# Spectral input of a two-layer GFNet kernel: five transposes of 128 columns, a plain copy of z, statistics one tile ahead

## The chip, the cores and the metric

The kernel runs on one core of a Trainium2 chip. Its time is the device time of one execution in microseconds (us), and lower is better. Three runs of the kernel before took 770.5, 771.51 and 773.9 us; the median is 771.51. The engines are called PE (TensorE; its weight loads, PEld, run beside its matmuls), DVE (VectorE), ACT (ScalarE), POOL (GpSimd) and SP (SyncE, which here only issues DMAs). Each engine works through its own queue of instructions in order.

## The reference

The input x has 2048 rows of 576 columns in bf16. Two layers are computed one after the other, each with its own residual additions:

```python
x = x + A(layernorm(x))          # spectral mixer
x = x + B(layernorm(x))          # MLP, which normalises its input once more

def A(x):   # X: 2048 x 289 complex
    X = rfft2(x) ; X = X * (w_r + 1j * w_i)
    return irfft2(X, s=(2048, 576))

def B(x):
    y = layernorm(x)
    return gelu(y @ w1 + b1) @ w2 + b2      # 576 -> 4608 -> 576
```

Both layers use the same weights. The transforms are done as matrix products with constant cosine and sine matrices.

## The kernel before

All of x stays in SBUF as 16 tiles; tile t holds the rows 16p + t on its 128 partitions p. The two-dimensional transform is done in factors. The real transform along the 576 columns comes first, tile by tile. The transform along the 2048 rows is split into 16 x 128 (in the code 8 and 16 inside a tile, then an exchange between partitions, then the rest). All instructions keep the order in which the program writes them down on each engine: a manual schedule is set for PE, ACT, DVE and POOL.

The class `SpectralIn` (from line 298) is the part that is changed. For each tile it does this:

- `fold` (lines 304 to 308): DVE adds and subtracts the two halves of the 576 columns, 288 each, into a buffer xf of two rows of 320. The sum serves the even frequencies, the difference the odd ones.
- Statistics: `ln_bn_one` (line 265) takes two batch statistics of 288 columns and one aggregation on DVE. `ln_scale` (line 271) makes 1/sqrt(variance + eps) from them. In the first stage ACT takes the square root (line 277) for two tiles at a time and DVE the reciprocal (line 280). In the MLP it is a chain of small DVE operations for one tile. The mean needs no subtraction at this place.
- `turn` (line 314): six PE transposes of 96 columns each (line 319), and one ACT copy of the 96 x 768 result out of PSUM (line 321) into xT.
- `dft_d` (line 324): six matmuls with 290 moving columns (line 329), three for the even and three for the odd frequencies, against the constant c_fd. ACT copies the result z (line 334), multiplies it by the row's 1/sqrt, and at the same time interleaves even and odd frequencies, writing every second element.
- `dft_v` (line 341): four matmuls (lines 344 to 347) with the constant c_k1 as weights and z as the moving operand, into two PSUM rows, real and imaginary. ACT (line 350) or DVE (line 352), in turn, copies the result to y1, which has 5 buffers.
- `exchange` (line 380): SP issues one DMA that spreads y1 over 8 partitions of the array vx. A buffer of y1 is free again when its DMA has read it.

The method `run_all` (line 356) is the first stage of layer 0. In iteration i it does `turn` of tile i-1, `dft_v` of tile i-4, `dft_d` of tile i-2, `fold` of tile i, then the statistics of tile i, and with every second tile the square root and the reciprocal of that pair. Constants and weights for the following stage are loaded by POOL (line 211) in the same iterations; each load waits for the `turn` copy of a given tile.

After this stage come `middle` (line 389: the second row factor, the multiplication by w, and the first factor of the way back), `SpectralOut` (line 450: the rest of the way back and the residual addition) and `mlp` (line 672). `middle` begins with a matmul that reads vx, so it needs all exchanges.

Layer 1's spectral input isn't a stage of its own. In the MLP of layer 0, `mlp_down` (line 652) finishes the rows of one tile after another, and calls hooks after every sixth of its matmuls' groups; `fold`, `turn`, `dft_d` and `dft_v` of the tile before are put into these hooks. So 15 tiles are worked on between MLP matmuls. The sixteenth follows after the last MLP matmul, with filler matmuls (`keep_busy`, line 202) between its steps.

Of the kernel before, what the change touches and what calls it, by code (L numbers as in the profile page):

```python
# [10 lines left out]
ACT = mybir.ActivationFunctionType  # L11
ALU = mybir.AluOpType
BF16 = mybir.dt.bfloat16
F32 = mybir.dt.float32
# [7 lines left out]
S, D = 2048, 576  # L22
P = 128
NT = 16
DH = D // 2
KH = 145
KP = 2 * KH
# [10 lines left out]
ENGINES = [getattr(mybir.EngineType, n) for n in ("PE", "Activation", "DVE", "Pool")]  # L38


def _fd():
    d = np.arange(DH)[:, None].astype(np.float64)
    j = np.arange(KH)[None, :].astype(np.float64)
    halves = []
    for odd in range(2):
        ang = 2 * np.pi * d * (2 * j + odd) / D
        re, im = np.cos(ang), -np.sin(ang)
        dead = KH - 1 if odd else 0
        re[:, dead] = 0
        im[:, dead] = 0  # L50
        halves.append(np.concatenate([re, im], axis=1).reshape(3, 96, KP))
    return np.concatenate(halves, axis=0).transpose(1, 0, 2)


def _k1():
# [61 lines left out]
def kernel(  # L117
# [12 lines left out]
    nc = tc.nc  # L130
# [5 lines left out]
    persist = ctx.enter_context(tc.tile_pool(name="persist", bufs=1))  # L136
    arena = ctx.enter_context(tc.tile_pool(name="arena", bufs=1))
    shared = ctx.enter_context(tc.tile_pool(name="shared", bufs=1))
    work = ctx.enter_context(tc.tile_pool(name="work", bufs=2))
# [5 lines left out]
    def uid():  # L145
        _n[0] += 1
        return _n[0]

    def big_ps(shape, dtype=F32):
        return ps_big.tile(shape, dtype, tag="big", name=f"psb{uid()}")  # L150

    def sm_ps(shape, dtype=BF16):
        return ps_sm.tile(shape, dtype, tag="sm", name=f"pss{uid()}")
# [13 lines left out]

    x_sb = persist.tile([P, NT, D], BF16, name="x_sb")
    ident = persist.tile([P, P], BF16, name="ident")
    c_fd = persist.tile([96, 6, KP], BF16, name="c_fd")  # L170
    c_k1 = persist.tile([P, 3, P], BF16, name="c_k1")
    c_f2 = persist.tile([P, 16, 3, P], BF16, name="c_f2")
    c_r1 = persist.tile([P, 2, 256], BF16, name="c_r1")
# [14 lines left out]
    order = [t for q in QUADS for t in q]  # L188
# [11 lines left out]
    marks = {}  # L200
# [64 lines left out]
    def ln_bn_one(mv, t):  # L265
        stats = work.tile([P, 2, nc.vector.BN_STATS_DIM], F32, tag="ln_stats")
        for h in range(2):
            nc.vector.bn_stats(out=stats[:, h, :], in_=x_sb[:, t, h * DH : (h + 1) * DH])  # L268
        nc.vector.bn_aggr(out=mv, in_=stats[:])  # L269

    def ln_scale(mv, mlp, sqrt):

        n = mv.shape[1]
        rs = work.tile([P, n], F32, tag="ln_rs", bufs=4)
        if sqrt:
            sq = work.tile([P, n], F32, tag="ln_v")
            nc.scalar.activation(
                out=sq[:], in_=mv[:, :, 1], func=ACT.Sqrt, bias=c_eps[:, 1:2] if mlp else c_eps[:, 0:1], scale=(1.0 + EPS) if mlp else 1.0
            )
            nc.vector.reciprocal(out=rs[:], in_=sq[:])  # L280
            return [(mv[:, i, 0:1], rs[:, i : i + 1]) for i in range(n)]

        vv = work.tile([P, n], F32, tag="ln_v")
        hv = work.tile([P, n], F32, tag="ln_hv")
        tt = work.tile([P, n], F32, tag="ln_t")
        sc, add = (1.0 + EPS, EPS * EPS) if mlp else (1.0, EPS)
        nc.vector.tensor_scalar(out=vv[:], in0=mv[:, :, 1], scalar1=sc, scalar2=add, op0=ALU.mult, op1=ALU.add)
        nc.vector.tensor_scalar(out=hv[:], in0=vv[:], scalar1=-0.5, scalar2=None, op0=ALU.mult)
        nc.vector.tensor_scalar(
            out=rs[:].bitcast(I32), in0=vv[:].bitcast(I32), scalar1=-0.5, scalar2=1597463007.0, op0=ALU.mult, op1=ALU.add  # L290
        )
        for _ in range(3):
            nc.vector.tensor_mul(out=tt[:], in0=rs[:], in1=rs[:])
            nc.vector.tensor_mul(out=tt[:], in0=tt[:], in1=hv[:])
            nc.vector.scalar_tensor_tensor(out=rs[:], in0=tt[:], scalar=1.5, in1=rs[:], op0=ALU.add, op1=ALU.mult)
        return [(mv[:, i, 0:1], rs[:, i : i + 1]) for i in range(n)]

    class SpectralIn:
# [3 lines left out]
            self.vx, self.st, self.sqrt = vx, {}, sqrt  # L302

        def fold(self, t, odd_engine):
            xf = work.tile([P, 2, 320], BF16, tag="xn", bufs=3)
            nc.vector.tensor_tensor(out=xf[:, 0, 0:DH], in0=x_sb[:, t, 0:DH], in1=x_sb[:, t, DH:D], op=ALU.add)  # L306
            odd_engine.tensor_tensor(out=xf[:, 1, 0:DH], in0=x_sb[:, t, 0:DH], in1=x_sb[:, t, DH:D], op=ALU.subtract)
            self.st["xf", t] = xf

        def stats(self, tiles):  # L310
# [2 lines left out]

        def turn(self, t):
            xf = self.st.pop(("xf", t))
            pt = sm_ps([P, 6, P])
            for o in range(2):
                for ci in range(3):
                    nc.tensor.transpose(pt[0:96, 3 * o + ci, :], xf[:, o, 96 * ci : 96 * ci + 96], ident[:])  # L319
            xT = work.tile([96, 6, P], BF16, tag="turn")  # L320
            marks["turn", t] = nc.scalar.copy(out=xT[:], in_=pt[0:96]).ins  # L321
            self.st["xT", t] = xT

        def dft_d(self, t):
            xT = self.st.pop(("xT", t))
            pz = big_ps([P, 2, 512])
            for o in range(2):
                for ci in range(3):
                    nc.tensor.matmul(  # L329
                        pz[:, o, 0:KP], lhsT=xT[:, 3 * o + ci, :], rhs=c_fd[:, 3 * o + ci, :],  # L330
                        start=(ci == 0), stop=(ci == 2),
                    )
            z = work.tile([P, 2, KP], BF16, tag="z", bufs=3)
            nc.scalar.activation(
                out=z[:].rearrange("p r (j o) -> p r o j", o=2),
                in_=pz[:, :, 0:KP].rearrange("p o (r j) -> p r o j", r=2),
                func=ACT.Copy, scale=self.st.pop(("rs", t)),
            )
            self.st["z", t] = z

        def dft_v(self, t, on_act):
            z = self.st.pop(("z", t))
            py = big_ps([P, 2, 512])
            nc.tensor.matmul(py[:, 0, 0:KP], lhsT=c_k1[:, 0, :], rhs=z[:, 0, :], start=True, stop=False)
            nc.tensor.matmul(py[:, 0, 0:KP], lhsT=c_k1[:, 2, :], rhs=z[:, 1, :], start=False, stop=True)
            nc.tensor.matmul(py[:, 1, 0:KP], lhsT=c_k1[:, 0, :], rhs=z[:, 1, :], start=True, stop=False)
            nc.tensor.matmul(py[:, 1, 0:KP], lhsT=c_k1[:, 1, :], rhs=z[:, 0, :], start=False, stop=True)
            y1 = work.tile([P, 2, KP], BF16, tag="y1", bufs=5)
            if on_act:
                ins = nc.scalar.copy(out=y1[:], in_=py[:, :, 0:KP]).ins  # L350
            else:
                ins = nc.vector.tensor_copy(out=y1[:], in_=py[:, :, 0:KP]).ins
            marks["y1", t] = ins
            exchange(self.vx, t, y1[:])

        def run_all(self, loads):
            for i in range(NT + 4):
                if 0 <= i - 1 < NT:
                    self.turn(order[i - 1])
                if 0 <= i - 4 < NT:  # L360
                    self.dft_v(order[i - 4], on_act=(i % 2 == 0))
                if 0 <= i - 2 < NT:
                    self.dft_d(order[i - 2])
                if i < 4:
                    keep_busy((5, 1, 1, 1)[i])
                if i < NT:
                    t = order[i]
                    self.fold(t, nc.vector)
                    if i % 2 == 0:
                        mv = work.tile([P, 2, nc.vector.BN_AGGR_DIM], F32, tag="ln_mv", bufs=4)  # L370
                    ln_bn_one(mv[:, i % 2, :], t)
                    if i % 2 == 1:
                        for tt, (_, rs) in zip(order[i - 1 : i + 1], ln_scale(mv, False, self.sqrt)):
                            self.st["rs", tt] = rs
                for call in loads.get(i, ()):
                    call()

# [160 lines left out]
    class Prep:  # L538
# [14 lines left out]
        def moments(self):  # L553
            mean = work.tile([P, 4], F32, tag="ln_hv")
            var = work.tile([P, 4], F32, tag="ln_v")
            sq = work.tile([P, 4], F32, tag="ln_t")
            nc.vector.tensor_scalar(out=mean[:], in0=self.s12[:, 0], scalar1=1.0 / D, scalar2=None, op0=ALU.mult)
            nc.vector.tensor_mul(out=sq[:], in0=mean[:], in1=mean[:])
            nc.vector.scalar_tensor_tensor(out=var[:], in0=self.s12[:, 1], scalar=1.0 / D, in1=sq[:], op0=ALU.mult, op1=ALU.subtract)
            self.mean, self.var = mean, var  # L560
# [157 lines left out]
    for n, (kind, j) in enumerate(first[:-3]):  # L718
        i = 1 + max(n - 1, 0)
# [72 lines left out]
```

## Time and profile before

| what | us |
|---|---|
| median of three runs (lowest, highest) | 771.51 (770.5, 773.9) |
| the profiled execution's own time | 772.16 |
| its span, first to last instruction | 770.4 |
| PE busy | 743.6 |
| ACT busy | 341.8 |
| DVE busy | 256.9 |
| first spectral stage, to the first matmul of `middle` | 0 to 46.5 |
| stretch with layer 1's spectral tiles inside the MLP | from about 150 to 412.9 |
| last tile of layer 1's spectral input, to the first matmul of `middle` | 414.8 to 423.2 |

Busy time is the sum over an engine's instructions, counted once where they overlap. The granted TensorE clock was full during the whole span. A row of the order of work shows the start, the duration, the engine, the line of the code, the operation, what it writes and reads, and in square brackets the idle time of the engine before it with what ended that idle time. A duration counts from start to end of one instruction; instructions of one engine overlap somewhat, so the distance between starts is what a queue of them costs.

### The profile page before, as it was taken

How to read it: one execution, taken by the hardware profiler on the slowest of the kernel's cores; microseconds unless marked ns; L12 is line 12 of the kernel's file. 1: busy time of each engine (PE TensorE's matmuls, PEld its weight loads, DVE VectorE, ACT ScalarE, POOL GpSimd, SP SyncE). 2: the span in 40 equal slices, each digit the busy share in tenths (PEclk: the TensorE clock that was granted, in tenths of full speed). 3: DMA queues.
4: the chain of work that ended last, by engine and by line, in shares of the span. 5: the costliest groups of instructions: out<-in, count | busy, mean ns of one | idle time of the engine just before them, and what ended most of it. 6: DMA issues, size and time to landing. Idle time of an engine off the chain costs nothing. (4 is left out here: it accounts for less than half of the span.)

```text
span 770.4 us, 12539 instructions
## 1 busy us (share of the span) xinstructions
PE 743.6 (97%) x5207; PEld 464.6 (60%) x5207; DVE 256.9 (33%) x843; ACT 341.8 (44%) x561; POOL 39.8 (5%) x75
## 2 busy tenths in 40 slices
PE   8879999999999999999999898999999999999997
PEld 5645744785478547854686565458646854784476
DVE  5855960245024602330133959201400140010011
ACT  6956855324542464236422866641154035204600
POOL 3320011000000000000004000100000000000000
PEclk9999999999999999999999999999999999999999
DMA  7844935000000000000004510620000000000000
GB/s 225 223 129 163 260 97 181 2 16 9 1 9 17 9 1 9 17 9 1 9 11 143 162 48 1 199 77 17 16 0 8 17 9 0 9 16 9 0 17 16
DMA packets 22377, 41.61 MB, mean 54 GB/s; under 512 B 4292, under 2 KB 15376, under 8 KB 22320
## 3 DMA queue, kind: packets, MB, share of 16 engines
q0 software_dynamic: 5696, 22.57, 9.7%
q1 hardware_dynamic: 16224, 17.76, 7.7%
q8 instruction: 41, 0.67, 0.4%
q10 hardware_dynamic: 400, 0.47, 0.2%
q14 instruction: 16, 0.13, 0.1%
HBM read 28.93 MB, written 2.36 MB: 41 GB/s over the span
## 5 line engine op out<-in xcount | busy, mean ns | idle before, releaser
L660 PEld LDWEIGHTS <-h_sb 128*128 128x128 bf16 x2304 | 223.8, 98 | 56.7
L618 PEld LDWEIGHTS <-w_sb 128*128 128x128 bf16 x1152 | 108.7, 98 | 145.8 <-issue 22.6
L590 DVE TENSOR_SCALAR xn<-x_sb,mv,rs 128x576 bf16<-128x576 bf16 x24 | 9.4, 427 | 198.1 <-PE pss_6918 L600 33.8
L268 DVE BATCH_NORM_STATS2 stats<-x_sb 128x6 f32<-128x288 bf16 x112 | 44.7, 440 | 0.0
L626 PEld LDWEIGHTS <-w1r_sb 64*128 64x128 bf16 x288 | 10.2, 94 | 26.0 <-issue 20.3
L656 DVE TENSOR_TENSOR xb<-x_sb,b_bc 128x576 f32<-128x576 bf16 x32 | 24.0, 749 | 0.0
L329 PEld LDWEIGHTS <-xT 96*128 96x128 bf16 x192 | 19.3, 101 | 7.0 <-ACT xT L321 0.7
L593 POOL COPY xn<-xn 128x64 bf16<-128x64 bf16 x24 | 5.8, 253 | 335.7 <-DVE xn L590 335.5
L319 PEld LDWEIGHTS <-xf 128*96 128x96 bf16 x192 | 15.4, 131 | 11.2 <-DVE xf L306 10.6
L428 PEld LDWEIGHTS <-h_sb 128*128 128x128 bf16 x128 | 12.0, 96 | 14.3 <-issue 9.5
L398 PEld LDWEIGHTS <-c_f_80 128*128 128x128 bf16 x128 | 12.3, 97 | 9.4 <-issue 5.1
L668 DVE TENSOR_TENSOR x_sb<-psb_7445,xb 128x576 bf16<-128x576 f32 x1 | 0.8, 758 | 43.6 <-PE psb_7445 L660 43.6
L668 DVE TENSOR_TENSOR x_sb<-psb_4074,xb 128x576 bf16<-128x576 f32 x1 | 0.8, 758 | 41.6 <-PE psb_4074 L660 41.6
L206 PEld LDWEIGHTS <-zeros 128*128 128x128 bf16 x86 | 8.5, 102 | 10.0 <-DVE h_sb L224 1.0
L211 POOL DMA_DIRECT2D h_sb<-in_A_w_r_dram x8 | 6.0, 750 | 133.3 <-issue 103.6
L269 DVE BATCH_NORM_AGGREGATE mv<-stats 128x2 f32<-128x12 f32 x56 | 11.7, 209 | 1.9
L600 PEld LDWEIGHTS <-xn 128*128 128x128 bf16 x160 | 11.5, 98 | 1.4
L632 ACT ACTIVATE h_sb<-psb_5977,b_sb 128x512 bf16<-128x512 f32 x2 | 1.3, 684 | 23.7 <-PE psb_5977 L626 23.7
L632 ACT ACTIVATE h_sb<-psb_7209,b_sb 128x512 bf16<-128x512 f32 x2 | 1.3, 684 | 23.7 <-PE psb_7209 L626 23.7
L632 ACT ACTIVATE h_sb<-psb_6593,b_sb 128x512 bf16<-128x512 f32 x2 | 1.3, 684 | 23.7 <-PE psb_6593 L626 23.7
L548 ACT ACTIVATE h_sb<-x_sb 128x576 bf16<-128x576 bf16 x16 | 11.0, 686 | 0.1
L306 DVE TENSOR_TENSOR xf<-x_sb 128x288 bf16<-128x288 bf16 x32 | 9.6, 299 | 4.1 <-DMA x_sb<-in_A_x_dram 4.1
(1353 smaller groups left out, 1478.4 us busy)
## 6 DMA issues: line engine op xcount, KB each, us to landing
w_sb<-in_B_w_dram SPq DMA_DIRECT2D x16, 288.0 KB
v_sb<-in_B_w_dram POOLq DMA_DIRECT2D x4, 1152.0 KB, 6.6
h_sb<-const_i POOLq DMA_DIRECT2D x8, 384.0 KB, 5.9
shared_1445<-in_B_w_dram POOLq DMA_DIRECT2D x2, 1440.0 KB, 7.3
shared_5356<-in_B_w_dram POOLq DMA_DIRECT2D x2, 1440.0 KB, 7.8
b_sb<-shared_704 SPq DMA_DIRECT2D x16, 145.0 KB
v_sb<-shared_4643 SPq DMA_DIRECT2D x16, 145.0 KB
h_sb<-in_A_w_r_dram POOLq DMA_DIRECT2D x8, 289.0 KB, 4.4
```

The costliest lines, as they stand in the source:

```text
L268: nc.vector.bn_stats(out=stats[:, h, :], in_=x_sb[:, t, h * DH : (h + 1) * DH])
L269: nc.vector.bn_aggr(out=mv, in_=stats[:])
L319: nc.tensor.transpose(pt[0:96, 3 * o + ci, :], xf[:, o, 96 * ci : 96 * ci + 96], ident[:])
L329: nc.tensor.matmul(pz[:, o, 0:KP], lhsT=xT[:, 3 * o + ci, :], rhs=c_fd[:, 3 * o + ci, :], start=(ci == 0), stop=(ci == 2),)
L398: nc.tensor.matmul(px[:, o, 0:KP], lhsT=c_f2[:, e, pl, :], rhs=vx[:, e, ri, :], start=(q == 0), stop=(q == 1))
L428: nc.tensor.matmul(ph[:, o, 0:KP], lhsT=i1[:, n % 4, pl, :], rhs=xp[:, ri, :], start=(q == 0), stop=(q == 1))
L548: nc.scalar.activation(out=at(h_sb, [P, D], 512 * 34), in_=x_sb[:, self.quad[i], :], func=(ACT.Copy, ACT.Square)[k], accum_out=self.s12[:, ...
L600: nc.tensor.transpose(pt[:, ci, :], xn[:, ci * 128 : (ci + 1) * 128], ident[:])
L618: nc.tensor.matmul(ph[:, q, :], lhsT=w1_sb[:, ci, fc * 128 : (fc + 1) * 128], rhs=yT[:, ci, :], start=(first and ci == 0), stop=(not first ...
L626: nc.tensor.matmul(acc[p][:, q, :], lhsT=w1r_sb[rows, p, :], rhs=yT[rows, 4, :], start=first, stop=not first)
L656: nc.vector.tensor_tensor(out=xb[:], in0=xr, in1=b2_bc[:].rearrange("p (h n) -> p h n", h=2), op=ALU.add)
L660: nc.tensor.matmul(po[:, h, 0:DH], lhsT=hts[fc][:, i * 128 : (i + 1) * 128], rhs=w2_chunk(fc)[:, h * DH : (h + 1) * DH], start=(fc == 0), ...
```

## The change

`fold` now writes xf as one run of 576 columns, sums then differences. `turn` transposes it in five pieces of 128 columns, at 0, 128, 256, 384 and 448; the last two overlap by 64 columns. The third piece holds both even and odd columns, so both groups of three matmuls in `dft_d` read it. The constant c_fd grows from 96 to 128 partitions and has zeros where a piece holds columns of the other half, or columns already counted.

The copy of z in `dft_d` keeps the order of PSUM: even frequencies, then odd ones, each with real and imaginary part. The moving operand of `dft_v` now reads z with an inner step of 290 elements (even, odd) and an outer step of 1. The output is the same interleaved order as before.

In `run_all` the fold of tile i comes directly after the transposes of tile i-1; after it, with every second tile, come the square root and the reciprocal; then `dft_v` and `dft_d`; and at the end of the iteration the statistics of tile i+1.

```diff
+CHUNKS = ((0, 0), (128, 0), (256, 0), (384, 0), (448, 64))
+HALF_CHUNKS = ((0, 1, 2), (2, 3, 4))
...
-    c_fd = persist.tile([96, 6, KP], BF16, name="c_fd")
+    c_fd = persist.tile([P, 6, KP], BF16, name="c_fd")
...
-            xf = work.tile([P, 2, 320], BF16, tag="xn", bufs=3)
-            nc.vector.tensor_tensor(out=xf[:, 0, 0:DH], in0=x_sb[:, t, 0:DH], in1=x_sb[:, t, DH:D], op=ALU.add)
-            odd_engine.tensor_tensor(out=xf[:, 1, 0:DH], in0=x_sb[:, t, 0:DH], in1=x_sb[:, t, DH:D], op=ALU.subtract)
+            xf = work.tile([P, 640], BF16, tag="xn", bufs=3)
+            nc.vector.tensor_tensor(out=xf[:, 0:DH], in0=x_sb[:, t, 0:DH], in1=x_sb[:, t, DH:D], op=ALU.add)
+            odd_engine.tensor_tensor(out=xf[:, DH:D], in0=x_sb[:, t, 0:DH], in1=x_sb[:, t, DH:D], op=ALU.subtract)
...
-            pt = sm_ps([P, 6, P])
-            for o in range(2):
-                for ci in range(3):
-                    nc.tensor.transpose(pt[0:96, 3 * o + ci, :], xf[:, o, 96 * ci : 96 * ci + 96], ident[:])
-            xT = work.tile([96, 6, P], BF16, tag="turn")
-            marks["turn", t] = nc.scalar.copy(out=xT[:], in_=pt[0:96]).ins
+            pt = sm_ps([P, 5, P])
+            for ci, (start, _) in enumerate(CHUNKS):
+                nc.tensor.transpose(pt[:, ci, :], xf[:, start : start + 128], ident[:])
+            xT = work.tile([P, 5, P], BF16, tag="turn")
+            marks["turn", t] = nc.scalar.copy(out=xT[:], in_=pt[:]).ins
...
-            nc.scalar.activation(
-                out=z[:].rearrange("p r (j o) -> p r o j", o=2),
-                in_=pz[:, :, 0:KP].rearrange("p o (r j) -> p r o j", r=2),
-                func=ACT.Copy, scale=self.st.pop(("rs", t)),
-            )
+            nc.scalar.activation(out=z[:], in_=pz[:, :, 0:KP], func=ACT.Copy, scale=self.st.pop(("rs", t)))
...
+            zk = z[:].rearrange("p o (r j) -> p r j o", r=2)
             py = big_ps([P, 2, 512])
-            nc.tensor.matmul(py[:, 0, 0:KP], lhsT=c_k1[:, 0, :], rhs=z[:, 0, :], start=True, stop=False)
-            nc.tensor.matmul(py[:, 0, 0:KP], lhsT=c_k1[:, 2, :], rhs=z[:, 1, :], start=False, stop=True)
-            nc.tensor.matmul(py[:, 1, 0:KP], lhsT=c_k1[:, 0, :], rhs=z[:, 1, :], start=True, stop=False)
-            nc.tensor.matmul(py[:, 1, 0:KP], lhsT=c_k1[:, 1, :], rhs=z[:, 0, :], start=False, stop=True)
+            for r, terms in enumerate((((0, 0), (2, 1)), ((0, 1), (1, 0)))):
+                for q, (pl, ri) in enumerate(terms):
+                    nc.tensor.matmul(
+                        py[:, r, 0:KP].rearrange("p (j o) -> p j o", o=2), lhsT=c_k1[:, pl, :], rhs=zk[:, ri], start=(q == 0), stop=(q == 1)
+                    )
...
         def run_all(self, loads):
+            pairs = {}
+
+            def moments(n):
+                if n % 2 == 0:
+                    pairs[n // 2] = work.tile([P, 2, nc.vector.BN_AGGR_DIM], F32, tag="ln_mv", bufs=4, name=f"mv{uid()}")
+                ln_bn_one(pairs[n // 2][:, n % 2, :], order[n])
+
             for i in range(NT + 4):
                 if 0 <= i - 1 < NT:
                     self.turn(order[i - 1])
+                if i < NT:
+                    self.fold(order[i], nc.vector)
+                    if i == 0:
+                        moments(0)
+                if i % 2 == 1 and i < NT:
+                    for tt, (_, rs) in zip(order[i - 1 : i + 1], ln_scale(pairs.pop(i // 2), False, self.sqrt)):
+                        self.st["rs", tt] = rs
                 if 0 <= i - 4 < NT:
                     self.dft_v(order[i - 4], on_act=(i % 2 == 0))
                 if 0 <= i - 2 < NT:
                     self.dft_d(order[i - 2])
                 if i < 4:
                     keep_busy((5, 1, 1, 1)[i])
-                if i < NT:
-                    t = order[i]
-                    self.fold(t, nc.vector)
-                    if i % 2 == 0:
-                        mv = work.tile([P, 2, nc.vector.BN_AGGR_DIM], F32, tag="ln_mv", bufs=4)
-                    ln_bn_one(mv[:, i % 2, :], t)
-                    if i % 2 == 1:
-                        for tt, (_, rs) in zip(order[i - 1 : i + 1], ln_scale(mv, False, self.sqrt)):
-                            self.st["rs", tt] = rs
+                if i + 1 < NT:
+                    moments(i + 1)
```

More of the change, by code (lines that the diff above doesn't have):

```diff
@@ L43, in _fd @@
     j = np.arange(KH)[None, :].astype(np.float64)
-    halves = []
-    for odd in range(2):
-        ang = 2 * np.pi * d * (2 * j + odd) / D
+    out = np.zeros((128, 6, KP))
+    for o in range(2):
+        ang = 2 * np.pi * d * (2 * j + o) / D
         re, im = np.cos(ang), -np.sin(ang)
-        dead = KH - 1 if odd else 0
+        dead = KH - 1 if o else 0
         re[:, dead] = 0
         im[:, dead] = 0
-        halves.append(np.concatenate([re, im], axis=1).reshape(3, 96, KP))
-    return np.concatenate(halves, axis=0).transpose(1, 0, 2)
+        m = np.concatenate([re, im], axis=1)
+        for q, ci in enumerate(HALF_CHUNKS[o]):
+            start, fresh = CHUNKS[ci]
+            for row in range(fresh, 128):
+                if o * DH <= start + row < (o + 1) * DH:
+                    out[row, 3 * o + q] = m[start + row - o * DH]
+    return out
 def _k1():
@@ L327, in dft_d @@
             for o in range(2):
-                for ci in range(3):
+                for q, ci in enumerate(HALF_CHUNKS[o]):
                     nc.tensor.matmul(
-                        pz[:, o, 0:KP], lhsT=xT[:, 3 * o + ci, :], rhs=c_fd[:, 3 * o + ci, :],
-                        start=(ci == 0), stop=(ci == 2),
+                        pz[:, o, 0:KP], lhsT=xT[:, ci, :], rhs=c_fd[:, 3 * o + q, :], start=(q == 0), stop=(q == 2),
                     )
             z = work.tile([P, 2, KP], BF16, tag="z", bufs=3)
-            nc.scalar.activation(
-                out=z[:].rearrange("p r (j o) -> p r o j", o=2),
-                in_=pz[:, :, 0:KP].rearrange("p o (r j) -> p r o j", r=2),
-                func=ACT.Copy, scale=self.st.pop(("rs", t)),
-            )
+            nc.scalar.activation(out=z[:], in_=pz[:, :, 0:KP], func=ACT.Copy, scale=self.st.pop(("rs", t)))
             self.st["z", t] = z
```

## The prediction

> **What bounds the kernel now.** I read the busy shares first, then tables of busy time by stretch, then the order of instructions inside the first stage, inside the multilayer perceptron (MLP) and at the hand-over between them.
>
> ```profile
> PE 743.6 (97%) x5207; PEld 464.6 (60%) x5207; DVE 256.9 (33%) x843; ACT 341.8 (44%) x561; POOL 39.8 (5%) x75
> 20.00:30.00 10.00, 8.63 (x77) 6.31 (x78) 8.67 (x29) 8.85 (x15) 3.75 (x5) 1.00 0.85 216
> 150.00:250.00 100.00, 100.00 (x735) 66.42 (x733) 34.12 (x140) 39.25 (x60) 0.99 (x4) 1.00 0.04 10
> ```
>
> The last two lines (after the stretch: PE, PEld, DVE, ACT, POOL, then clock, DMA share, GB/s) separate two regimes. In the MLP of layer 0, 15 of layer 1's 16 spectral tiles are slipped between matmuls while PE is never idle: there only PE time counts, and what DVE or ACT saves is worth nothing. In the first stage (0 to 46 us) four things are nearly equal. Its order of work over one pair of tiles:
>
> ```profile
> 28.79 0.81 DVE L268 BATCH_NORM_STATS2 stats<-x_sb 128x6 f32<-128x288 bf16 x2
> 29.64 0.21 DVE L269 BATCH_NORM_AGGREGATE mv<-stats 128x2 f32<-128x12 f32 x1
> 29.88 0.30 ACT L277 ACTIVATE sq<-mv,c_eps 128x2 f32<-128x2 f32 x1 [0.27 <-DVE mv L269]
> 30.21 0.17 DVE L280 RECIPROCAL rs<-sq 128x2 f32<-128x2 f32 x1 [0.36 <-ACT sq L277]
> 30.29 0.29 DVE L306 TENSOR_TENSOR xf<-x_sb 128x288 bf16<-128x288 bf16 x1
> 30.76 0.64 ACT L350 CAST y_514<-psb_509 128x580 bf16<-128x580 f32 x1
> 31.30 0.92 ACT L334 ACTIVATE z<-psb_517,rs 128x580 bf16<-128x580 f32 x1
> ```
>
> The next pair's fold starts at 32.43 and the one before at 28.36: 4.07 us a pair, 2.04 a tile. DVE is idle only for the 0.36 before the reciprocal: DVE's work plus the round trip to ACT's square root is the cycle. DVE alone would need 4.07 - 0.36 = 3.71 a pair, 1.85 a tile. PE's starts in one tile (30.63 transposes, 31.06 first k1 matmul, 31.55 first DFT matmul, then 6 x 0.123) add up to 1.66. The exchange transfers come next:
>
> ```profile
> 39.00:40.00 1.00, 0.61 (x6) 0.41 (x5) 0.75 (x1) 1.00 (x3) 0.00 (x0) 1.00 0.51 156
> 42.00:43.00 1.00, 1.00 (x7) 0.49 (x6) 0.59 (x1) 0.01 (x1) 0.00 (x0) 1.00 0.52 179
>   DVE y_701 L352: 2.4, 1
> ```
>
> With the loads gone the DMA share stays near 0.5 until 45.5, and the third line (who waited for the exchange's issues) says that the last y1 copy waited for the transfer that frees its buffer. In the packet records of the SP queue the exchanges run end to end: the last five begin at 40.83, 41.71, 42.49, 43.53 and 44.53, and the last ends at 45.70.
>
> [...] The new moving operand takes alternately one element from each of two runs 580 B apart[...]. The trace has no such moving operand (its matmuls read runs or a step of 0): unseen. [...] 128x512 from PSUM takes 587 ns as a copy, 684 with a bias pointer. [...]
>
> **The change, part by part.**
>
> *Five transposes.* In the MLP six start 0.056 apart (406.37 to 406.87, the last lasting 0.22). One fewer in 15 tiles: -0.84 on PE, on the path. The eviction becomes 128x640: 0.69 by line 602's copies, for 0.78 to 0.80. The matmuls of dft_d stay six of 290 columns; 128 rows for 96 cost no column.
>
> *Plain z.* 0.64 (the y1 copy, same size) + 0.09 (pointer) = 0.73 for 0.92; bounds 0.64 and 0.92. In the MLP hidden under PE; in the last tile -0.19 on the path; in stage 1 ACT work that does not bind.
>
> *Interleave in the matmul access.* Four matmuls a tile, lines 344 to 347:
>
> ```profile
> 411.87 0.29 PE L344 MATMUL psb_4555<-z,c_k_79 128*128 128x290 bf16 x1
> 411.99 0.29 PE L345 MATMUL psb_4555<-z,c_k_79 128*128 128x290 bf16 x1
> 412.12 0.28 PE L346 MATMUL psb_4555<-z,c_k_79 128*128 128x290 bf16 x1
> 412.24 0.29 PE L347 MATMUL psb_4555<-z,c_k_79 128*128 128x290 bf16 x1
> ```
>
> They start 0.123 apart. The lower bound for the new ones is that same 0.123 (no gain is possible: same columns). [...] I take twice, 0.246[...]. In the MLP 15 x 4 x 0.123 = +7.4, with nothing to hide it, since PE is the bound.
>
> *Last tile of the MLP (414.8 to 423.2), a bare chain* fold, transposes, eviction, DFT, z, k1, y1, exchange: -0.06 - 0.11 - 0.19 + 0.49 = +0.13.
>
> *Statistics one tile ahead.* Nothing is added but the order: DVE now does fold i, (reciprocal, y1 copy), then moments of i+1; ACT's square root stands between eviction and z. Steady state: the pair's sums are ready before the fold, so the square root's answer comes while DVE folds: the 0.36 goes, leaving 1.85 a tile. But at the start DVE's moments of the next tile wait for its load, ahead of that tile's fold: x arrives for 5.22, 8.72, about 10. The 1.0 of moments (0.81 + 0.21) that stood behind each fold stands in front: the third and fourth folds go from 8.72 and 10.14 to about 9.7 and 11.2, and PE, in order, is that late too. The larger c_fd (326 to 435 KB, about 0.4 at the 290 GB/s of 2 to 6 us) adds up to 0.4 to x's arrival. While DVE waits for such a load, its queued fold is late, and with it the transposes, which stand ahead of the k1 and DFT matmuls in PE's queue. So +1.4 until something has slack to catch up.
>
> With doubled k1 matmuls PE needs 5 x 0.062 + 4 x 0.246 + 6 x 0.123 = 2.03 a tile: DVE's slack is used up by PE, the pace stays 2.04 and the +1.4 is kept. The POOL loads are paced by the evictions and move with them; 12 of them end long before the middle stage.
>
> Sum: +7.4 - 0.84 + 0.13 + 1.4 = +8.1, on the profiled execution's 772.16: 780.3. The median of the runs lies 0.65 lower, so 779.6.
>
> **Rivals.**
>
> *A, no penalty on the strided read, and the exchanges hold stage 1 back* (not slower). MLP -0.84, last tile -0.36. In stage 1 DVE gains about 0.2 a tile, makes up the start by the seventh fold (about 17.7 in both) and is some 2.2 earlier at the end. But on its eight engines a transfer needs 0.9 and a 384 KB load about 1.2 (at twice the 160 GB/s that half of the engines show), together 2.1 a tile against 1.85: the chain, end to end in the records above, can't follow. I grant it 0.6: 771.5 - 1.8 = 769.7. [...]
>
> *B, no penalty and the exchanges do follow*: -0.84 - 0.36 - 2.2 = -3.4, 768.1. Against it: the wait for the transfer shown above.
>
> *C[...].* [...] At three times it is 7.4 x 2 - 0.84 + 0.6 + 8 = +22, 794.
>
> The forecast decides against A where the new spacing exceeds about 0.145 (the point at which 60 matmuls eat 1.3).
>
> **How the numbers follow.** About twice 0.42, A 0.24, B 0.08, three times and more (C) 0.26. The twofold case's own range is 775 to 785. Leaving out the best half of B's spread and the far half of C: 767.5 to 800. A difference under 0.5% (3.9 us) is about what a measurement of this kernel can't tell from none: 767.7 to 775.4 holds A, most of B, and a penalty below about 1.5 times: 0.33. Faster, B with more luck at the start: 0.07. Slower: 0.60.
>
> **What would show it.** Matmuls reading z spaced 0.246 instead of 0.123 ([...] A: 0.123). The MLP's stretch, from the first gelu to the last tile's fold, longer by 6.5. z at 0.73, the eviction at 0.69, five transposes. In stage 1: no wait before the reciprocal, fold 3 about 1 us late, PE close to fully busy from 20 to 38; in A instead DVE near full and y1 copies waiting for transfers. I am wrong if the k1 spacing is unchanged; then all hangs on the exchange chain. I am also wrong if the strided read slows the weight loads beside it or if z's copy doesn't get faster, though that one costs under 1 us.

## The result

The changed kernel took 781.46 us (median of 4 runs, 780.17 to 781.73) against 771.87 for the kernel before (median of 4 runs, one more than above): a ratio of 1.0119, 95% interval 1.0093 to 1.0144. A second measurement of the changed kernel gave 1.0102 (1.0078 to 1.0126). It is slower by about 1%, as forecast; 779.6 had been predicted.

Busy time by engine, and by stretch of time, of the kernel after. The columns are those of the same rows of before: PE, PEld, DVE, ACT, POOL, granted clock, DMA share, GB/s.

```profile
PE 753.8 (97%) x5175; PEld 461.9 (59%) x5175; DVE 255.9 (33%) x843; ACT 334.4 (43%) x561; POOL 39.8 (5%) x75
20.00:30.00 10.00, 10.00 (x76) 6.11 (x75) 8.80 (x30) 8.52 (x15) 3.57 (x6) 1.00 0.84 228
150.00:250.00 100.00, 100.00 (x709) 63.86 (x707) 31.56 (x134) 37.91 (x60) 0.99 (x4) 1.00 0.03 8
```

There are 32 matmuls fewer (two passes of 16 tiles, one transpose less each) and PE is busy 10.2 us longer. From 20 to 30 us PE is now busy all the time, where it was busy for 8.63 of the 10. In the MLP PE is full as before, but gets through fewer instructions in 100 us: 709 recorded in place of 735.

The order of work around the four k1 matmuls of one tile in the MLP, after:

```profile
155.83 1.17 PE L352 MATMUL psb_1922<-z,c_k_79 128*128 128x290 bf16 x4
156.08 0.10 PEld L352 LDWEIGHTS <-c_k_79 128*128 128x128 bf16 x1 [0.15 <-issue]
156.34 0.10 PEld L352 LDWEIGHTS <-c_k_79 128*128 128x128 bf16 x1 [0.15 <-issue]
156.84 0.53 PE L674 MATMUL psb_1806<-shared_1429,h_sb 128*128 128x288 bf16 x3
```

From the first k1 matmul to the next MLP matmul 1.01 us pass: 0.253 for each of four, where it was 0.123. The weight loads still take 0.10 and now wait 0.15 for their turn, so it isn't they that became slow; the matmul beside them is.

In the first stage, over one pair of tiles:

```profile
28.66 0.81 DVE L279 BATCH_NORM_STATS2 stats<-x_sb 128x6 f32<-128x288 bf16 x2
30.99 0.25 DVE L317 TENSOR_TENSOR xf<-x_sb 128x288 bf16<-128x288 bf16 x1
31.63 0.31 ACT L288 ACTIVATE sq<-mv_488,c_eps 128x2 f32<-128x2 f32 x1
31.97 0.17 DVE L291 RECIPROCAL rs<-sq 128x2 f32<-128x2 f32 x1 [0.51 <-ACT sq L288]
32.45 0.74 ACT L343 ACTIVATE z<-psb_550,rs 128x580 bf16<-128x580 f32 x1 [0.51 <-PE psb_550 L339]
```

The copy of z is at 0.74, and ACT waits for PE before it. The next pair starts at 32.73: 4.07 us a pair, the pace of before, but now it is PE's, which is never idle here. The matmul that opens the middle stage starts at 46.37 (before: 46.53).

Where the time went, as differences of starts taken from the order of work (from the first spectral transposes in the MLP to the last tile's fold, and from there to the first matmul of the second middle stage). The last two columns are two profiles of the changed kernel. The ends of the MLP stretch, two lines of before and two of after:

```profile
149.48 0.50 PE L319 MATMUL pss_1878<-ident,xf 128*96 128x128 bf16 x6
414.83 0.31 DVE L306 TENSOR_TENSOR xf<-x_sb 128x288 bf16<-128x288 bf16 x1
150.11 0.44 PE L329 MATMUL pss_1862<-ident,xf 128*128 128x128 bf16 x5
422.24 0.31 DVE L317 TENSOR_TENSOR xf<-x_sb 128x288 bf16<-128x288 bf16 x1
```

| stretch | before | after | after, again |
|---|---|---|---|
| start to first middle stage | 46.53 | 46.37 | 45.57 |
| MLP with 15 spectral tiles | 265.35 | 272.13 | 272.13 |
| last tile to second middle stage | 8.34 | 8.85 | 8.56 |

The first profile of after also lost 0.8 in the first middle stage, at its last exchange (from 26.97 to 27.75); the second didn't (26.97), so the change doesn't bring it with it every time. From the second middle stage to the end both need the same: 347.2 before, 347.3 after.

### The profile page after: what moved, and what is told of

The parts are those of the page before. It is cut to its first block, busy times and chain, and to the rows that moved or that the text cites. A ratio compares the mean times of both kernels' runs of the same rounds, so it can differ in the third digit from the quotient of the medians.

```text
span 778.4 us, 12473 instructions
## 1 busy us (share of the span) xinstructions
PE 753.8 (97%) x5175; PEld 461.9 (59%) x5175; DVE 255.9 (33%) x843; ACT 334.4 (43%) x561; POOL 39.8 (5%) x75
## 5 line engine op out<-in xcount | busy, mean ns | idle before, releaser
L640 PEld LDWEIGHTS <-w1r_sb 64*128 64x128 bf16 x288 | 10.2, 94 | 26.0 <-issue 20.3
L339 PEld LDWEIGHTS <-xT 128*128 128x128 bf16 x192 | 19.2, 101 | 9.6 <-issue 2.5
L352 PEld LDWEIGHTS <-c_k_79 128*128 128x128 bf16 x128 | 12.1, 99 | 11.3 <-issue 9.9
L412 PEld LDWEIGHTS <-c_f_80 128*128 128x128 bf16 x128 | 12.3, 97 | 9.3 <-issue 5.1
L329 PEld LDWEIGHTS <-xf 128*128 128x128 bf16 x160 | 11.9, 102 | 6.7 <-DVE xf L317 4.7
L305 DVE TENSOR_TENSOR tt<-tt,hv 128x1 f32<-128x1 f32 (+1 forms) x63 | 10.1, 160 | 2.2
```

Of the source, the lines that this page charges most:

```text
L329: nc.tensor.transpose(pt[:, ci, :], xf[:, start : start + 128], ident[:])
L339: nc.tensor.matmul(pz[:, o, 0:KP], lhsT=xT[:, ci, :], rhs=c_fd[:, 3 * o + q, :], start=(q == 0), stop=(q == 2),)
L352: nc.tensor.matmul(py[:, r, 0:KP].rearrange("p (j o) -> p j o", o=2), lhsT=c_k1[:, pl, :], rhs=zk[:, ri], start=(q == 0), stop=(q == 1))
L412: nc.tensor.matmul(px[:, o, 0:KP], lhsT=c_f2[:, e, pl, :], rhs=vx[:, e, ri, :], start=(q == 0), stop=(q == 1))
L640: nc.tensor.matmul(acc[p][:, q, :], lhsT=w1r_sb[rows, p, :], rhs=yT[rows, 4, :], start=first, stop=not first)
```

## The experiments

Ratios are to the kernel before, run beside each version.

**The interleave back in the copy of z**, with the five transposes and the new order kept.

```diff
-            nc.scalar.activation(out=z[:], in_=pz[:, :, 0:KP], func=ACT.Copy, scale=self.st.pop(("rs", t)))
+            nc.scalar.activation(
+                out=z[:].rearrange("p r (j o) -> p r o j", o=2),
+                in_=pz[:, :, 0:KP].rearrange("p o (r j) -> p r o j", r=2),
+                func=ACT.Copy, scale=self.st.pop(("rs", t)),
+            )
...
-                        py[:, r, 0:KP].rearrange("p (j o) -> p j o", o=2), lhsT=c_k1[:, pl, :], rhs=zk[:, ri], start=(q == 0), stop=(q == 1)
+            nc.tensor.matmul(py[:, 0, 0:KP], lhsT=c_k1[:, 0, :], rhs=z[:, 0, :], start=True, stop=False)
...
```

> The changed kernel with one part undone: ACT interleaves z again while copying it, and the four k1 matmuls read z in one run; five transposes and the statistics one tile ahead stay. Theory (the moving operand[...] is read at half rate, and nothing else costs): k1 matmuls start 0.123 us apart again instead of 0.253, the MLP stretch with spectral tiles is 7.8 us shorter than in the changed kernel and 0.8 shorter than in the kernel before; time 769 to 771.5. Rival (the five transposes with overlapping pieces or the new order cost as well): the time stays above 774.

Measured: 770.0 us, ratio 0.9977 (0.9965 to 0.9988). The MLP stretch is 264.44, that is 7.69 less than in the changed kernel and 0.91 less than before. So the interleave in the matmul access is worth 7.69 us there, 0.128 for each of 60 matmuls, and the rest of the change costs nothing. This version is 0.2% faster than the kernel before.

**The interleave alone**, put into the kernel before.

```diff
-                out=z[:].rearrange("p r (j o) -> p r o j", o=2),
-                in_=pz[:, :, 0:KP].rearrange("p o (r j) -> p r o j", r=2),
+            nc.scalar.activation(out=z[:], in_=pz[:, :, 0:KP], func=ACT.Copy, scale=self.st.pop(("rs", t)))
...
-            nc.tensor.matmul(py[:, 0, 0:KP], lhsT=c_k1[:, 0, :], rhs=z[:, 0, :], start=True, stop=False)
+                        py[:, r, 0:KP].rearrange("p (j o) -> p j o", o=2), lhsT=c_k1[:, pl, :], rhs=zk[:, ri], start=(q == 0), stop=(q == 1)
...
```

> The kernel before with the plain copy of z and the interleave in the access of the k1 matmuls alone; six transposes and the old order of statistics. Theory: k1 matmuls 0.253 us apart, 60 of them in the MLP stretch: +7.8 us there; the last tile +0.3; in the first stage PE needs 0.4 + 1.01 + 0.74 = 2.15 us a tile against a pace of 2.04: +1 to +2; so 780 to 783. Rival (the new order is what costs): below 776.

Measured: 783.66 us, ratio 1.0157 (1.0133 to 1.0181). The MLP stretch is 273.03, +7.68 on before: the same amount from the other side. The middle stage opens at 48.73, +2.2, a little over the expectation, and the median lies 0.7 above its upper end. With six transposes and the old order the first stage does get longer: a pair of tiles takes 4.76 us there (folds at 23.91 and 28.67) against 4.07 in the changed kernel, and PE, busy for 9.37 us from 20 to 30, waits for folds. In the changed kernel the other two parts pay for it. The transpose saved is worth 2 x 0.056 = 0.11 a pair, so most of the 0.69 between the two is the new order's; that split is worked out, not measured by itself.

**The new order of the first stage alone.**

```diff
+                if i < NT:
+                    self.fold(order[i], nc.vector)
...
-                if i < NT:
-                    t = order[i]
-                    self.fold(t, nc.vector)
...
+                if i + 1 < NT:
+                    moments(i + 1)
```

> The kernel before with the new order of the first stage alone (fold first, statistics one tile ahead). Theory of the exchange chain: the wait of DVE before the reciprocal goes and the folds come 1.85 to 1.95 us apart, but ACT with its 0.78 and 0.92 copies and the chain of exchange transfers keep the start of the middle stage at 45.5 to 46.5 us; time 770.5 to 772. Rival (DVE's cycle sets the end of the stage): middle starts before 45 us, time below 770. Second rival (the start is late by 1.4 us, as forecast): middle starts after 47.5.

Measured: 772.41 us, ratio 1.001 (0.9996 to 1.0025): no difference, though the middle stage opened at 45.18 in the profiled execution, a bit earlier than the expectation had it, and the median lies 0.4 above its upper end. The second rival, a late start by 1.4 us, is out. The MLP stretch is 265.34, as it must be. In this stage executions of one and the same kernel differ by a microsecond or two (44.01 and 45.89 further down), so one profile doesn't show a gain that the timed runs don't.

**Two halves in place of element by element.** The plain z is kept, and so are the sizes of all instructions; only the order in which the k1 matmuls take the elements changes. The later stages then combine the wrong frequencies.

```diff
-            zk = z[:].rearrange("p o (r j) -> p r j o", r=2)
+            zk = z[:].rearrange("p o (r j) -> p r o j", r=2)
...
-                        py[:, r, 0:KP].rearrange("p (j o) -> p j o", o=2), lhsT=c_k1[:, pl, :], rhs=zk[:, ri], start=(q == 0), stop=(q == 1)
+                        py[:, r, 0:KP].rearrange("p (o j) -> p o j", o=2), lhsT=c_k1[:, pl, :], rhs=zk[:, ri], start=(q == 0), stop=(q == 1)
```

> The changed kernel, but each k1 matmul reads z as two runs of 145 elements instead of alternately from both, so the frequencies leave in another order and the later stages combine wrong ones: the computation differs in that, all instructions have the same sizes. Theory [...]: 0.123 us apart as for one run, time 768.5 to 771. Rival (a moving operand of more than one run, or the plain layout of z, costs by itself): above 0.2 us apart, time near 781.

Measured: 770.07 us, ratio 0.998 (0.9963 to 0.9998); MLP stretch 264.47. The order of work on PE in that kernel:

```profile
154.27 0.66 PE L352 MATMUL psb<-z,c_k 128*128 128x290 bf16 x4
154.77 1.63 PE L674 MATMUL psb<-shared,h_sb 128*128 128x288 bf16 x12
```

Four in 0.50 us, 0.125 each. So neither the layout of z nor a moving operand of two runs costs anything: the alternation at every element does.

**The moving access by itself.**

> Not the task's computation: a kernel that copies x to the output and otherwise runs 24 matmuls of 288 or 290 moving columns (256 in one case) for each of 17 ways to read the moving operand, weights changing each time. Theory [...]: one run, runs of 8, 4 and 2 elements, two halves, and steps of 2 and 4 elements start 0.123 us apart; steps of 8 and more elements, and one element from each of two runs in turn, 0.25. Rival (any access with more than one run, or a step other than 1, is slow): runs of 2 and 4 and steps of 2 and 4 are slow too. Second rival (only the hop by hundreds of bytes is slow): steps of 8 and 16 are at full rate.

One execution. The order of work on PE, merged by line; each row is 24 matmuls of one access, so the distance to the next row's start, divided by 24, is the cost of one. (L93, where each element is read twice, ran while the clock rose, and isn't used.)

```profile
21.01 3.12 PE L54 MATMUL pk<-z,w 128*128 128x290 bf16 x24
23.97 6.24 PE L57 MATMUL pk<-z,w 128*128 128x290 bf16 x24
30.05 6.72 PE L60 MATMUL pk<-z,w 128*128 128x288 bf16 x24
36.61 3.84 PE L63 MATMUL pk<-z,w 128*128 128x288 bf16 x24
40.29 4.65 PE L66 MATMUL pk<-z,w 128*128 128x288 bf16 x24
44.77 3.21 PE L69 MATMUL pk<-z,w 128*128 128x288 bf16 x24
47.82 3.10 PE L72 MATMUL pk<-z,w 128*128 128x288 bf16 x24
50.76 3.14 PE L75 MATMUL pk<-z,w 128*128 128x290 bf16 x24
53.74 3.27 PE L78 MATMUL pk<-z,w 128*128 128x290 bf16 x24
56.84 6.35 PE L81 MATMUL pk<-z,w 128*128 128x290 bf16 x24
63.01 12.44 PE L84 MATMUL pk<-z,w 128*128 128x290 bf16 x24
75.27 12.70 PE L87 MATMUL pk<-z,w 128*128 128x290 bf16 x24
87.78 11.86 PE L90 MATMUL pk<-z,w 128*128 128x290 bf16 x24
99.47 4.35 PE L93 MATMUL pk<-z,w 128*128 128x290 bf16 x24
```

| moving operand (bf16) | line | us each | against one run |
|---|---|---|---|
| one run | 54 | 0.123 | 1 |
| one element in turn from two runs, 580 B apart (as in the change) | 57 | 0.253 | 2.05 |
| the same, 576 B apart | 60 | 0.273 | 2.2 |
| two elements in turn | 63 | 0.153 | 1.24 |
| two in turn, from an odd element on | 66 | 0.187 | 1.5 |
| four in turn | 69 | 0.127 | 1.03 |
| eight in turn | 72 | 0.123 | 1 |
| two halves | 75 | 0.124 | 1 |
| step of 2 elements | 78 | 0.129 | 1.05 |
| step of 4 | 81 | 0.257 | 2.1 |
| step of 8 | 84 | 0.511 | 4.1 |
| step of 16 | 87 | 0.521 | 4.2 |
| step of 64 | 90 | 0.487 | 4.0 |

The price in the change is reproduced. The theory is half right. Steps: the time for a column doubles from a step of 2 (0.129) to 4 (0.257) and again to 8 (0.511), then stays about the same (0.521, 0.487). Steps of 4 had been expected at full rate and steps of 8 at 0.25. A step of 8 elements is 16 bytes, so the rows of steps 2, 4 and 8 fit a price of about 1.76 ns (0.511 / 290) for each stretch of 16 bytes that is entered, whether one, two or four of its elements are used; that is an estimate from these rows, no row shows such stretches by themselves. Alternation: one element in turn costs 0.253, about as expected, and not 0.511, so a hop between two runs is half as dear as steps of 8 along one; why wasn't determined. Two in turn, expected at full rate, cost 0.153, and four 0.127. The granted clock fell to 0.5 during the matmuls with a step of 8, but they took 689 to 690 ns both ahead of the fall and after it. The steps of 16 and 64 ran at 0.5 throughout, all rows above the step of 8 at 1.

**Two queues for the exchanges**, on top of the version with the interleave back in the copy of z (from here on, the first version).

```diff
-            exchange(self.vx, t, y1[:])
+            exchange(self.vx, t, y1[:], nc.sync if on_act else nc.gpsimd)
...
-        ins = nc.sync.dma_start(out=dst[p0 : p0 + 29 : 4], in_=src).ins
+        ins = engine.dma_start(out=dst[p0 : p0 + 29 : 4], in_=src).ins
```

> The version with the interleave back in the copy of z, and in the first stage every second exchange is issued by POOL in place of SP, so that two exchanges can be under way at once. Theory (in that version the chain of exchange transfers on one queue sets the end of the stage): y1 copies no longer wait 3 us for a transfer, the middle stage starts at 43.5 to 45 in place of 45.9, and the time is 768 to 769.5. Rival (the memory system, or the loads that share the DMA engines, set the pace, not the queue): middle starts at 45.5 or later, 770 or more.

Measured: 769.38 us, ratio 0.997 (0.996 to 0.9981); the middle stage opens at 45.1. The time fits the theory, the start of the middle stage lies between the two; one y1 copy still waits 1.8 us for a transfer, and the interval overlaps that of the version with one queue. Inconclusive.

**Eight buffers for y1**, on top of the first version. The occasion was this row of the first version's order of work, where ACT stands still for 3.03 us before a y1 copy ("issue": the profile names nothing that it waited for). In the packet records of the SP queue of that version the exchanges run end to end from 19.63 to 45.27, and one of them ends at 33.53, just before the copy starts.

```profile
33.84 0.64 ACT L359 CAST y<-psb 128x580 bf16<-128x580 f32 x1 [3.03 <-issue]
```

```diff
-            y1 = work.tile([P, 2, KP], BF16, tag="y1", bufs=5)
+            y1 = work.tile([P, 2, KP], BF16, tag="y1", bufs=8)
```

> The version with the interleave back in the copy of z, and eight buffers for y1 in place of five. Theory (the transfers themselves are the chain): the copies of y1 stop waiting for a buffer, but the transfers run end to end as before and the middle stage starts within 0.4 us of 45.9; the time stays at 769.5 to 770.5. Rival (it is the wait for a buffer that delays the stage): middle starts before 45, time below 769.5.

Measured: 770.07 us, ratio 0.9971 (0.996 to 0.9983). The waits for a buffer are gone, but the middle stage opened at 43.0 in the profile, against the expectation. So the changed kernel, the first version and the one with eight buffers were measured again, side by side.

> The changed kernel unaltered, for a second profile and a narrower interval. Theory: k1 matmuls 0.253 us apart, the MLP stretch as in its first profile; the middle stage, which took 27.7 us in the first profile and 27.0 in that of the kernel before and of four others, takes 27.0 again if the 0.7 was chance in the landing of its last exchange; ratio 1.010 to 1.014.

Measured: 779.94 us, ratio 1.0102 (1.0078 to 1.0126); stretches in the table above.

> The version with the interleave back in the copy of z, unaltered, beside the next one. Middle stage starts at 45 to 46.5 us; ratio 0.9965 to 0.9988 as before.

Measured: 770.06 us, ratio 0.9974 (0.9962 to 0.9987); MLP stretch 264.43; the middle stage opened at 44.01, earlier than expected.

> The version with the interleave back in the copy of z and eight buffers for y1, unaltered, beside the one with five. If the wait for a buffer was part of what held the exchanges back, the middle stage starts at 42.5 to 44 us again and the median lies 1 to 3 us below that with five buffers; if the 43.0 of its first profile was chance, both start and time are within 0.6 us of the one with five.

Measured: 769.74 us, ratio 0.9972 (0.996 to 0.9985); it opened at 44.53, half a microsecond after the one with five buffers. So the 43.0 was chance: in the first version that start was at 45.89 and 44.01, and with eight buffers at 43.0 and 44.5, and the times are the same. Waiting for a buffer is not what sets the end of the stage. That the transfers themselves do is what the packet records suggest: they run end to end at the end of all four profiles, and the last five took 6.7 us together in the one that opened at 45.89, but 4.6, 4.2 and 4.4 in the other three. What made them longer isn't known, and no run here shortened them at will, so it is argued and not shown.

## Why the prediction was right

- **Interleave in the matmul access: +7.4 forecast in the MLP, +7.69 measured.** That the hop at every element slows the matmul, the place and the factor of two were right; 0.253 came for 0.246. That the factor was so close is partly luck: twice was the author's estimate, and no matmul of the trace of before has such an operand from which it could be derived. Steps of 8 and more along one run cost about four times (0.487 to 0.521 for 0.123), in rival C's range of three times and more; the hop between two runs costs half of that.
- **Five transposes: -0.84 forecast, -0.90 measured** (265.34 to 264.44, and 273.03 to 272.13). The parts add up without remainder: 265.35 + 7.68 - 0.90 = 272.13. The DFT matmuls, now on 128 rows for 96, start 0.123 apart as before (six take 0.91 us in both kernels, from 31.55 before and from 29.47 after).
- **Plain z: 0.73 forecast, 0.74 measured**, which is 0.10 more than the 0.64 of the y1 copy of the same size; the 0.09 for the pointer was the author's estimate, beside 0.10 between the 587 ns of a cast and the 684 of a gelu with a bias. The eviction came at 0.69 as forecast. Plain z bought nothing in the MLP, where ACT waits (264.47 with it and two halves, 264.44 without).
- **Last tile: +0.13 forecast, +0.51 and +0.22 measured.** The matmuls' +0.52 is there. From fold to k1 0.21 was gained instead of 0.36, because filler matmuls stand ahead of the k1 matmuls on PE (from 424.76; the k1 matmuls start at 425.85) and z was done before they were (at 425.70). The rest of the 0.51 is the landing of the exchange, 0.2 later in one profile and 0.1 earlier in the other.
- **First stage: +1.4 forecast, -0.16 and -0.96 measured. This step failed.** The pace was right: 2.04 a tile, PE full. Where PE doesn't bind, the forecast's 1.85 nearly came too (second profile of the first version: three pairs from 20.72 to 32.07, 1.89 a tile). The late start didn't come. The third fold started at 8.63 and 8.96 us in the two profiles, and at 8.99 with the new order alone, not at 9.7. Before, and two lines of after:

```profile
8.72 0.31 DVE L306 TENSOR_TENSOR xf<-x_sb 128x288 bf16<-128x288 bf16 x1 [1.47 <-DMA x_sb<-in_A_x_dram]
7.65 0.82 DVE L279 BATCH_NORM_STATS2 stats<-x_sb 128x6 f32<-128x288 bf16 x2 [0.55 <-DMA x_sb<-in_A_x_dram]
8.63 0.26 DVE L317 TENSOR_TENSOR xf<-x_sb 128x288 bf16<-128x288 bf16 x1
```

  Counted from the arrival of its load the delays are as forecast: the third fold comes 0.98 after it (at once in the old order), the fourth 2.35 (1.42). But that load arrived for 7.65, 7.98 and, with the new order alone, 8.01, not 8.72. With the interleave alone, in the old order, it came for 8.20, so one profile isn't enough to fix the time of a load. Whether it comes earlier because of the change (it was there by 8.01 in all nine profiles of the new order) or by chance, two profiles of the old order can't tell. The larger c_fd shows at the second tile, about as forecast: its load arrived for 5.47 to 5.69 in all eight profiles with it, and by 5.22 in the three without. At the third tile nothing of that is left.
- **No wait before the reciprocal** was forecast; it is there, 0.51, since ACT's square root comes after a copy that waits for PE. It costs nothing, as DVE has slack (busy for 8.80 us from 20 to 30, PE for 10.00).

The sum, +8.1, met +8.0 in the profiled execution partly by luck: 1.6 us too much for the first stage, and against it 0.8 of chance in the middle stage and 0.6 in the terms that were too small. Without the interleave in the matmul access, rival A's 769.7 is close to the measured 770.0 and 770.06, and B's 768.1 isn't. Their starts of the middle stage can't be told apart: 45.89 is A's gain of 0.6, 44.01 rather B's 2.2. A's threshold of 0.145 isn't derived (A's whole gain of 1.8 over 60 matmuls gives 0.153); with 0.253 nothing hangs on it. The eight engines that rival A gives an exchange are an estimate from the DMA share of 0.51 and 0.52 of 16 engines with the loads gone (before, 39 to 40 and 42 to 43 us); which engines carry an exchange isn't shown.

## What to carry to other kernels

A rearranged access costs an engine no instruction, but it can cost its rate (here 0.253 for 0.123): the place for an interleave is where an idle engine pays (here ACT, 0.18 us a tile, covered in the MLP), not the operand of the engine that is the bound. Before moving one, measure the access alone, 24 repetitions were enough here, and look at how many elements it takes in a row (one in turn cost 2.05 times as much as a run, two 1.24, four 1.03) and at its step (2 elements 1.05, 4 2.1, 8 4.1). Where one stretch is set by one engine and another by several at once, cost the change in each by itself; the first could be forecast here to some 5%, the second not within a microsecond, because loads and exchanges took other times in every profile (the third tile's load came for 7.47 to 8.72 where DVE waited for it; the last five exchanges took 4.2 to 6.7 in the four profiles above).

## What the hardware showed that was not expected

- With the moving access by itself, a bf16 operand of 290 columns with a step of 8, 16 or 64 elements ran at about a quarter of the rate (0.511, 0.521 and 0.487 for 0.123), with 4 at half (0.257), with 2 at 0.95 (0.129); alternating between two runs, at half (0.253). Taking four elements at a time from each of two runs was almost free (0.127). The price of alternation didn't add to that of a slow PE: in the first tile, where the k1 matmuls of the kernel before start 0.24 apart at a granted clock of 1.00, the alternating ones start 0.26 apart.
- Writing PSUM with a step of 2 fp32 elements cost almost as much in that run: matmuls of 256 columns start 0.214 apart (103.66 to 108.80) and 0.111 without a step.

```profile
103.66 5.34 PE L96 MATMUL pk<-z,w 128*128 128x256 bf16 x24
108.80 2.82 PE L99 MATMUL pk<-z,w 128*128 128x256 bf16 x24
111.46 3.12 PE L102 MATMUL pk<-z,w 128*128 128x290 bf16 x24
```

- The same kernel's times spread over 6 us (before: 769.78 to 775.96 in 43 runs), 0.8%; the mean granted clock of those runs went from 0.99 to 1.00, and the longer ones are mostly those with the lower clock (0.996 and less: 772.25 to 775.96; 0.999 and more: 769.78 to 773.26).
